# Reordering three stretches of a fused sparse-attention and bilinear feed-forward kernel on one NeuronCore

## Chip, cores and metric

One core of one Trainium2 chip runs the whole kernel. The metric is device time in microseconds (us). Engines are called as in the profile: PE (TensorE matmul), PEld (its weight loads), DVE (VectorE), ACT (ScalarE), POOL (GpSimd), SP (SyncE).

## What is computed

Inputs q, k, v have shape (8 batches, 8 heads, 576 positions, 64). Heads 0 to 3 see the last 32 positions ("local"), heads 4 to 7 see every earlier position with the same remainder modulo 32 ("strided"). The result, 4608 tokens of 512 numbers, goes through a feed-forward layer with a product instead of a nonlinearity.

```python
mask_local = (rel >= 0) & (rel < stride)                    # stride = 32
mask_strided = (rel >= 0) & (pos[None, :] % stride == pos[:, None] % stride)
scores = np.where(masks[None, :, :, :], scale * q @ k.T, -1000000000.0)
attn = softmax(scores)
x = (attn @ v).transpose(0, 2, 1, 3).reshape(B * S, H * D)
return (x @ w_a) * (x @ w_b) @ w_out                        # d_ff = 1536
```

## The kernel before

**Tiles.** The feed-forward layer runs over nine tiles t = 0 to 8 of 512 tokens. A tile has 16 slots: twelve `ffn_ab` (one block f of 128 of the 1536 middle columns each: eight matmuls of 512 columns, L546; ACT copies the a half, L563; DVE multiplies it with the b half into `pf`, L566 or L568) and four for the output multiplication. Attention of batch b lies between these slots, by the tables STEPS and LATER: in tile t of 2 to 6 the fifth values' step V5 of batch t+1 stands behind slot 11. The engines' instructions are issued in the order in which the program emits them (a manual schedule), so an instruction that waits holds all behind it on its engine.

**Output multiplication of tiles 2 to 8.** It is a fast matrix scheme with seven products of half size in place of eight; each product is, for q = 0 and 1, six matmuls of 256 columns (groups g = 0 to 5), accumulated in four PSUM banks a, b, c, d. The products are named 1 to 7. Products 3 and 4 read `pf` as it is. The others read sums of `pf` pieces, tile `ps`, five planes of six groups:

- plane 0, the diagonal sum, `fast_s(t, 0, ...)`, L579, read by product 1;
- planes 1 and 2, one instruction for both, `fast_s(t, 1, ...)`, L581, read by product 5 (plane 1) and product 2 (plane 2);
- planes 3 and 4, `fast_s(t, 2, ...)`, L583, read by products 6 and 7.

In tiles 2 to 7 (`y_plan`, matmuls at L650) the order is 3 4 1 7 5 2 6, each for both q. Groups 0 and 1 of the sums are made in earlier slots; groups 2 to 5 of the diagonal sum are emitted in slot 11, behind V5, whose last DVE part is two multiplications into xT (L471) that wait for two ACT steps (L464, L465). Groups 2 to 5 of planes 1 and 2 follow in slot 12. In tile 8 (`y_tail`, matmuls at L678) all seven products are done for q = 0 and then for q = 1, in the order 3 4 1 2 5 6 7. After product 4 of q = 0 comes `fast_s` for planes 1 and 2 of the last group, after product 1 that for planes 3 and 4. Product 2 accumulates onto bank b, product 5 onto a, 6 onto c. Behind product 2 ACT copies its bank (L693) and POOL subtracts it from the running sum (L694); behind product 5 the same at L698 and L699; behind 6 and 7 DVE finishes output quarters (L703, L706), which SP and ACT queues store.

**The first batch.** Batch 0 is worked through before any slot, in an order written out by hand, the string ORDER (L507). The steps are, for head pair c and unit u (units 0 to 3 local, 4 to 7 strided):

- Tk*c*p / Tq*c*p: PE transposes k or q (L264, L270); Tk*c*e by DVE (L281) and Tq*c*e by ACT (L285) copy them out;
- S*u*p: PE score product (L357; strided units first add the mask with two matmuls, L351), into the one buffer `st`; S*u*x: ACT exponential (L365); S*u*m: DVE mask (L375), local units only;
- V*u*p: PE product with v (L411), into one of two `o` banks; V*u*r and V*u*n: DVE reciprocal and multiplication (L419, L434), which set the bank free;
- X*c*p / X*c*e: PE transposes the result (L480), ACT or DVE copies it into xT (L496; X3: L493 and L494);
- G0 to G2: the strided mask on PE, DVE and POOL (G1 also issues many of POOL's loads); F0a to F1c: parts of the first two `ffn_ab`; Z: an ACT fill; *n: n filler matmuls (`spin`, L154).

S5, "the sixth score product", is unit 5; V2 and V3 are the last local values' products. POOL issues nearly all loads, in program order; weights come in `load_w` (L244) and `load_wo` (L247).

The softmax here doesn't subtract the row's maximum and nothing guards it: scores larger than these inputs give would overflow.

## Time and profile before

| | before |
|---|---|
| median of 4 runs | 333.03 us (332.79 to 338.19) |
| profiled execution: time, span | 332.82 us, 330.8 us |
| mean granted PE clock | 0.999 |
| PE busy | 324.5 us, 98% of the span |
| DVE, ACT, POOL busy | 80%, 61%, 53% |

The profiled execution's time is its span and 2.0 us around it. A timeline row is: start (us from the span's start), us from the first start to the last end, engine, line, operation, written tile <- read tiles, sizes, count, and in brackets how long the engine was idle before and what ended that. Instructions of one kind in a row are merged into one row. Matmuls overlap: a row of n matmuls lasts n - 1 start-to-start steps and one full duration.

### The profile page before, as it was taken

Reading aid. Unit: us, or ns where it says so; the run is one execution under the profiler, and the core shown is the slowest. Engines: PE = TensorE matmul, PEld = TensorE weight load, DVE = VectorE, ACT = ScalarE, POOL = GpSimd, SP = SyncE. Lnnn points to the kernel's source line nnn. Section 1 sums busy time; section 2 is a strip of 40 time slices with the busy share of each in tenths; the row PEclk is TensorE's granted clock in tenths of the full one; section 3 lists DMA queues with packets and bytes.
Section 4 is the critical chain, followed back from the end, with each engine's and each line's share of the span. In section 5 each row is a group of like instructions: output and inputs, shape, how many; then the busy total and the mean of one; then the engine's idle time right before and its main releaser. Section 6 shows DMA issues by size and latency. Waiting matters only on the chain.

```text
span 330.8 us, 7724 instructions
## 1 busy us (share of the span) xinstructions
PE 324.5 (98%) x2850; PEld 205.3 (62%) x2850; DVE 263.8 (80%) x500; ACT 201.9 (61%) x328; POOL 175.9 (53%) x296
## 2 busy tenths in 40 slices
PE   8999999999999999999999999999999999999995
PEld 6654555455555577556999985558555854584464
DVE  6867587778877999999999999999878845647662
ACT  5662956468777866787577757775777543313321
POOL 8946746399966655774577557854312031132021
PEclk9999999999999999999999999999999999999999
DMA  9999999599999599799898988998033022004004
GB/s 157 142 202 194 202 186 198 125 184 117 131 199 141 98 97 81 73 199 141 77 83 174 158 85 70 140 207 88 22 76 113 0 65 64 0 2 127 3 0 127
DMA packets 100662, 37.60 MB, mean 114 GB/s; under 512 B 77457, under 2 KB 97809, under 8 KB 100625
## 3 DMA queue, kind: packets, MB, share of 16 engines
q0 software_dynamic: 87760, 19.58, 64.8%
q1 hardware_dynamic: 12576, 17.34, 18.0%
q8 instruction: 22, 0.36, 0.5%
q10 hardware_dynamic: 288, 0.20, 0.2%
q14 instruction: 16, 0.12, 0.2%
HBM read 39.71 MB, written 9.44 MB: 149 GB/s over the span
## 4 chain that ended last, share of the span: by engine, by line
PE 81%; DMA 11%; POOL 4%; DVE 1%; issue 1%; POOLq 0%; ACT 0%; DVEq 0%
PE mm L546 50%; PE mm L650 17%; DMA vl<-in_v_dram 4%; PE mm L730 4%; PE o L455 4%; PE st L357 4%; DMA shared<-in_k_dram 3%; DMA wa_sb<-in_moe_w_a_dram 3%; PE mm L678 1%; POOL shared L196 1%; DMA natk<-in_k_dram 1%; POOL vl L223 1%; PE end L678 1%; POOL wa_sb L244 0%; DVE tk L300 0%
## 5 line engine op out<-in xcount | busy, mean ns | idle before, releaser
L546 PE MATMUL mm<-xT,wb_sb 128*128 128x512 bf16 (+1 forms) x472 | 110.3, 358 | 0.1
L546 PE MATMUL mm<-xT,wa_sb 128*128 128x512 bf16 (+1 forms) x472 | 110.4, 358 | 0.0
L563 ACT COPY a_sb<-mm 128x512 f32<-128x512 f32 x106 | 62.0, 585 | 49.0 <-PE mm L546 46.8
L546 PEld LDWEIGHTS <-wb_sb 128*128 128x128 bf16 x480 | 46.3, 98 | 44.5 <-issue 0.6
L879 POOL CAST pace<-pf 1x1 f32<-1x1 bf16 x84 | 29.2, 347 | 83.2 <-DVE pf L566 80.8
L566 DVE TENSOR_TENSOR pf<-a_sb,mm 128x512 bf16<-128x512 f32 x84 | 56.4, 671 | 17.0 <-PE mm L546 13.7
L546 PEld LDWEIGHTS <-wa_sb 128*128 128x128 bf16 x480 | 42.5, 98 | 31.3
L365 ACT ACTIVATE p<-st 128x576 bf16<-128x576 f32 (+1 forms) x64 | 41.6, 650 | 11.0 <-PE st L357 10.3
L464 ACT ACTIVATE xr<-o 64x576 f32<-64x576 f32 x48 | 31.1, 647 | 26.3 <-PE o L455 26.1
L650 PEld LDWEIGHTS <-ps 128*128 128x128 bf16 x360 | 34.1, 98 | 5.3 <-DVE ps L579 1.5
L465 ACT ACTIVATE xr<-xr 64x576 f32<-64x576 f32 x48 | 32.8, 683 | 1.5
L471 DVE TENSOR_TENSOR xT<-o,xr 64x288 bf16<-64x288 f32 x48 | 21.5, 447 | 8.0 <-ACT xr L465 7.0
L469 DVE TENSOR_TENSOR xT<-o,xr 64x288 bf16<-64x288 f32 x48 | 21.4, 446 | 7.5 <-ACT xr L465 7.0
L650 PE MATMUL mm<-wf,ps 128*128 128x256 bf16 x216 | 27.3, 273 | 0.1
L375 DVE TENSOR_TENSOR p<-p,mask_l 128x576 int16<-128x576 int16 x32 | 22.3, 698 | 2.8 <-ACT p L365 2.8
L730 PE MATMUL mm<-wo_sb,pf 128*128 128x512 bf16 x96 | 23.4, 379 | 0.0
L235 POOL DMA_DIRECT2D vs<-in_v_dram x24 | 19.6, 818 | 4.0 <-PE st L357 3.7
L568 DVE TENSOR_TENSOR pf<-a_sb,mm 128x512 bf16<-128x512 f32 x22 | 14.9, 676 | 7.5 <-ACT a_sb L563 5.9
L879 POOL COPY pace<-y_sb 1x1 f32<-1x1 f32 x16 | 2.8, 175 | 32.0 <-ACT y_sb L633 14.8
L211 POOL DMA_DIRECT2D ql<-in_q_dram x24 | 16.0, 665 | 5.7 <-DMA wo_sb<-in_moe_w_out_dram 3.7
L211 POOL DMA_DIRECT2D kl<-in_k_dram x24 | 16.1, 671 | 4.0 <-issue 3.8
L650 PE MATMUL mm<-wf,pf 128*128 128x256 bf16 x144 | 17.6, 273 | 0.0
(151 smaller groups left out, 501.7 us busy)
## 6 DMA issues: line engine op xcount, KB each, us to landing
out_dram<-y_sb SPq DMA_DIRECT2D x12, 512.0 KB, 5.1
vl<-in_v_dram POOLq DMA_DIRECT2D x7, 384.0 KB, 7.0
out_dram<-y_sb SPq DMA_DIRECT2D x10, 256.0 KB, 4.0
kl<-in_k_dram POOLq DMA_DIRECT2D x24, 72.0 KB, 3.4
ql<-in_q_dram POOLq DMA_DIRECT2D x24, 72.0 KB, 3.5
vs<-in_v_dram POOLq DMA_DIRECT2D x24, 72.0 KB, 3.6
wo_sb<-in_moe_w_out_dram POOLq DMA_DIRECT2D x4, 384.0 KB, 11.7
natk<-in_k_dram POOLq DMA_DIRECT2D x20, 72.0 KB, 3.4
```

Of the source, the lines that this page charges most:

```text
L211: nc.gpsimd.dma_start(out=t[32 * h:32 * h + 32], in_=src[b, h].rearrange("(i y) d -> y i d", y=32))
L365: nc.scalar.activation(p[:M, :, :W], st[:M, :, :W], ACT.Exp, scale=scale)
L375: nc.vector.tensor_tensor(pi, pi, mk, op=ALU.bitwise_and)
L464: nc.scalar.activation(r, sums, ACT.Ln)
L465: nc.scalar.activation(r, r, ACT.Exp, scale=-1.0)
L471: nc.vector.tensor_mul(dst.rearrange("d (p r) -> d p r", r=RS)[:, :, G * half:G * (half + 1)], o[:64, j, :W].rearrange("d (g p) -> d p g", ...
L546: nc.tensor.matmul(ps_[:, c0:c0 + n], lhsT=w[:, kk, 128 * f:128 * (f + 1)], rhs=xT[:, kk, x0:x0 + n], start=(kk == first and c0 == 0), sto ...
L563: nc.scalar.copy(a_sb, ab[0])
L566: nc.vector.tensor_mul(pf[:, f, :].rearrange("p (i a s) -> p a i s", i=2, s=16), halves(a_sb), halves(ab[1]))
L650: nc.tensor.matmul(bank[b][:, q], lhsT=lhs(g, q), rhs=rhs(g), start=new and q == 0 and g == 0, stop=g == FG - 1, skip_group_check=True)
L730: nc.tensor.matmul(y, lhsT=pf[:, f, 128 * j:128 * (j + 1)], rhs=wo_sb[:, f], start=(f == 0), stop=(f == FD - 1))
L879: nc.gpsimd.tensor_copy(pace, done)
```

## The change

Three orders are changed; nothing is computed differently and no instruction but fillers is added or removed. (1) In ORDER, V0n, S5p, S5x, X0p and X0e come before V2p; V2's and V3's steps, S6p, V4, X1p and V5p follow in a new order; G2 goes behind Tk2e; fillers go from *2 to *4 behind Tk0p, from *2 to *1 ahead of S4p, *2 are added ahead of V2p, and the *1 ahead of V7p and the *1 ahead of F0b go. (2) In tiles 2 to 7 the diagonal sum of groups 2 to 5 is emitted before the attention step behind slot 11. (3) In tile 8, q = 0, product 5 comes before product 2.

```diff
-        V1p S0m *2 S2p V1r S3m V0p S2x Tk3p V0r Tk3e *2 S4p S2m Tq3p S4x V1n Tq3e *4 V2p V0n S5p V2r V3p V2n S5x X0p V4p V3r
-        V3n X0e S6p V4r V5p V4n S6x X1p V5r S7p X1e V5n V6p S7x X2p V6r *1 V7p V6n X2e Z F0a V7r V7n *1 F0b X3p F1a X3e F0c
+        V1p S0m *2 S2p V1r S3m V0p S2x Tk3p V0r Tk3e *1 S4p S2m Tq3p S4x V1n Tq3e *4 V0n S5p S5x X0p X0e *2 V2p V2r V3p V2n
+        S6p V4p V3r V3n V4r V4n S6x X1p V5p V5r S7p X1e V5n V6p S7x X2p V6r V7p V6n X2e Z F0a V7r V7n F0b X3p F1a X3e F0c
...
-            for k in "3412567":
+            for k in ("3415267", "3412567")[q]:
...
+        soon = {16 * t + 11: [lambda t=t: fast_s(t, 0, slice(2, 6))] for t in FAST_Y[:-1]}
...
-            for slot, n, z0, z1 in ((4, 0, 0, 2), (6, 2, 0, 2), (8, 1, 0, 2), (10, 2, 2, 4), (11, 0, 2, 6), (11, 2, 4, 6),
+            for slot, n, z0, z1 in ((4, 0, 0, 2), (6, 2, 0, 2), (8, 1, 0, 2), (10, 2, 2, 4), (11, 2, 4, 6),
...
+            for f in soon.get(i, ()):
+                f()
             take(i)
```

## The prediction, made before the changed kernel was run

> **What bounds the kernel now.** I read the page's busy times first, then the waits of PE and PEld, then the timeline where those waits lie.

> ```profile
> PE 324.5 (98%) x2850; PEld 205.3 (62%) x2850; DVE 263.8 (80%) x500; ACT 201.9 (61%) x328; POOL 175.9 (53%) x296
> ...
> PEld L650 <- DVE ps L579: 1.5, 5, 0.3
> PEld L678 <- DVE ps L581: 0.5, 1, 0.5
> ```

> PE is busy for 98% of the span, and from 60 us on hardly anything keeps it waiting, so a reordering can only win the few waits left: five weight loads of product 1 waiting for the diagonal sum, one in the last tile, and what the first batch leaves. Those rows total the loader's idle time; what PE itself loses is read from the timeline. Tile 3, PE, then DVE:

> ```profile
> 190.77 1.24 PE L650 MATMUL mm<-wf,ps 128*128 128x256 bf16 x8
> 192.10 1.92 PE L650 MATMUL mm<-wf,ps 128*128 128x256 bf16 x16
> 193.85 0.71 PE L650 MATMUL mm<-wo_sb,ps 128*128 128x256 bf16 x5
> ...
> 188.65 0.68 DVE L566 TENSOR_TENSOR pf<-a_sb,mm 128x512 bf16<-128x512 f32 x1
> 189.48 0.91 DVE L471 TENSOR_TENSOR xT<-o,xr 64x288 bf16<-64x288 f32 x2 [0.16 <-ACT xr L465]
> 190.43 0.69 DVE L579 TENSOR_TENSOR ps<-pf 128x1024 bf16<-128x1024 bf16 x1
> 192.64 1.18 DVE L581 TENSOR_TENSOR ps<-pf 128x2048 bf16<-128x2048 bf16 x1
> ```

> Sixteen matmuls take 1.92 us, five 0.71: 0.11 each. Eight should take 0.71 + 3 x 0.11 = 1.04; product 1's first eight take 1.24. **0.20 is lost**, because the sum ends at 190.43 + 0.69 = 191.12, behind V5's L471. The last tile, products 1, 2 and 5, 6 on PE, then DVE:

> ```profile
> 318.43 0.82 PE L678 MATMUL mm<-wf,ps 128*128 128x256 bf16 x6
> 319.51 1.49 PE L678 MATMUL mm<-wo_sb,ps 128*128 128x256 bf16 x12 [0.27 <-DVE ps L581]
> 320.83 1.47 PE L678 MATMUL mm<-wf,ps 128*128 128x256 bf16 x12
> ...
> 319.04 0.42 DVE L581 TENSOR_TENSOR ps<-pf 128x512 bf16<-128x512 bf16 x1
> ```

> Six steps of 0.11 from 318.43 let product 2 start at 319.09; it starts at 319.51: **0.42 lost**. The start:

> ```profile
> 14.06 0.34 PE L411 MATMUL o<-vl,p 128*128 128x65 bf16 x6 [0.44 <-DMA vl<-in_v_dram]
> 14.24 0.41 PE L351 MATMUL st<-nmask,ident 72*128 72x288 bf16 x2
> 14.96 0.65 ACT L365 ACTIVATE p<-st 72x576 bf16<-72x576 f32 x1 [1.02 <-PE st L357]
> ...
> 47.01 1.67 PE L730 MATMUL mm<-wo_sb,pf 128*128 128x512 bf16 x6
> 49.26 1.46 PE L730 MATMUL mm<-wo_sb,pf 128*128 128x512 bf16 x6
> ```

> V2p at 14.06 waits for v, and S5p (14.24) and its exponential stand behind it. At 47.01 six matmuls take 0.21 more than six of the same kind at 49.26: the last quarter of w_out, issued by POOL at 34.89 with 12.9 us to landing (the longest of the four), lands at 47.8.

> **Diagonal sum first.** The sum reads block 11 of `pf`, so it starts when L566 ends, about 189.37 (in the last tile L579 starts 0.72 after L566, 317.39 to 318.11). It ends at 190.06, before product 1 begins at 190.77: the 0.20 goes, in the five tiles that the wait row counts, 1.0 in all. Queued behind it are V5's two L471, which move from 189.48 to 189.98 (step between neighbours 0.61) and end 0.5 later, at 190.9; they free bank o for V6's product, which starts at 191.84 now and about 191.6 then: 0.6 of cover, and what it lacks would be lost per tile. DVE loses its 0.16 idle, so L581 ends at about 193.72 instead of 193.82. Product 5 needs it at its third matmul, weights loaded from 193.96, then 193.76 at the earliest: just enough. I take 0.95 of the 1.0.

> [...] L579 at 190.43 lasts 0.69 and the next starts at 191.04, after 0.61, so here neighbours overlap by 0.08 and the row decides. [...]

> **Last tile.** L581 writes group 5 of planes 1 and 2 in one instruction. Product 2's first weight load already waits for it, though it reads group 0 of plane 2. Product 1's loads begin at 318.32, before L579's end at 318.40, so the wait isn't on the whole tile; it fits a wait on the range of addresses from the first to the last written, and plane 2's first groups lie within. Plane 1's groups 0 to 4 lie ahead of it, so product 5 can start at 319.09, and its sixth load comes at about 319.53, after L581's end at 319.46. The 0.42 goes. POOL then works for product 5 first and product 2 second, ready at about 321.8 (two of 0.7, from 320.4), so L703 slips from 321.74 to about 321.9; L706 at 322.40 is hardly touched, and the quarters of q = 0 are stored long before the last store. The end follows q = 1, whose order is the same: 0.42, less nothing. If the wait is for the tile after all, 0.

> **First batch.** Fillers: five take 0.67 and four 0.56, so 0.1 each at this clock; two more put Tq0p and all behind it 0.2 later, to V0p at 11.41. There Tk3p waits for k anyway (11.61, 0.17 idle on the loader): the 0.2 vanishes but for 0.1 on S4p, which waits for S2x. S5p then starts when S4x ends (12.77 + 0.1 + 0.65), 13.55 instead of 14.24. S5p takes 0.58 (14.24 to 14.82 now), X0p 0.37, two fillers 0.2: V2p starts at 14.70 instead of 14.06, **0.64 later**. From it V2n ends 1.16 on (15.86), V3n at 16.56. V4p waits for V2's bank (15.91), X1p and V5p for V3n (16.61); X1p 0.36 and V5p 0.44 give S7p at 17.41 instead of 17.20, and V7p, by S7's exponential, about 18.87 instead of 18.61. The score products' lead is eaten: S6p comes 0.8 earlier, but the values' chain on DVE is later and sets the end. One filler fewer behind V7p leaves F0c, and with it the tiles, **0.18 late** (bounds: 0, and the whole 0.64). G2's move hides behind Tk2p, for which Tk2e waits.

> PE's later waits up to 47 us are for DVE and ACT and move along; the one at 47.01 is for a landing. POOL's queue keeps it: the v loads behind V5p and V7p (18.15, 19.50) come 0.3 later at most, and POOL then idles 1.17 before 21.34. So lateness up to 0.21 costs nothing, and an earlier start would gain nothing either. I take 0, with 0 to 0.64 - 0.21 = +0.43.

> On the fillers' price: 23 at the very start take 4.45 us, 0.185 each, five from 6.59 on 0.10; I took 0.10, since the added ones come after 6 us. [...]

> **Sum.** -0.95 - 0.42 + 0 = -1.37. The profiled execution, 332.82, becomes 331.45; the median of the runs lies 0.21 above it (one run of 338.19 in it), so I say **331.6**.

> **Rivals.** *The wait moves to L581* (0.14): its slack at product 5 is 0.09 today (193.87 against 193.96); if DVE doesn't close its 0.16 idle, four tiles gain 0.09 each and only the sixth, where no transpose stands before L581, 0.2: 0.56 in place of 0.95, 332.0. *Product 5 waits as well* (0.09): the change doesn't do what it says in the tail, +0.42, 332.0; for it speaks that both planes come from one instruction, against it product 1's early loads. *The first batch is later than the cover* (0.13): +0.43, 332.0; for it the two o banks, which chain V2 to V7. *Slower* (0.07): the PE clock stays at half longer in the first batch, since its gaps change. Each us of PE work then costs 0.85 more (0.185 against 0.10). A start late by x costs x - 0.21, so it decides from x = 1.6, about 1.9 us of PE work at half clock, and with 3.0 us of it (x = 2.5) gives 332.82 - 1.37 + 2.3 = 333.8. Against it: fillers cost 0.10 throughout from 6 us, and gaps there are below 0.7.

> **Numbers.** My forecast has 0.57. About 0.2% (0.67 us) is what a measurement tells from no change. Below 332.4 lie the forecast and most of three rivals: faster 0.81. Two of the +0.4 cases together give about 332.4, and part of the start's lateness more: same 0.12. Slower 0.07. Low end: both full gaps (1.42) off the lowest run, 331.4, less 0.2 for run to run: 331.2. High end: two rivals at once, 332.4, and 0.1: 332.5.

> **What would show it.** Right: no wait on L579 at L650; product 1's eight in 1.04; last tile's product 5 starting 0.66 after product 1; F0c near 22.0 and the w_out wait gone or shorter; V2p near 14.7. Wrong: a wait on L581 at L650 or on V6's bank, F0c past 22.1 with PE behind after 48, or fillers of 0.185 after 6 us.

## The result and the profile after

The changed kernel took 331.95 us (median of 32 runs, 330.8 to 336.92) against 332.89 us for the kernel before (51 runs). The ratio is 0.997, 95% interval 0.9957 to 0.9983: 0.94 us faster, by the interval 0.6 to 1.4. The forecast was 331.6, range 331.2 to 332.5. Ratios here compare runs without a longer disturbance; each run's mean granted PE clock is told where it is part of the finding.

The profiled execution took 330.8 us with a span of 328.8, 2.0 less than before. The page's busy times, and the row on L471 of the waits of PEld:

```profile
PE 322.4 (98%) x2851; PEld 205.4 (62%) x2851; DVE 264.3 (80%) x500; ACT 202.1 (61%) x328; POOL 177.5 (54%) x296
...
PEld L455 <- DVE xT L471: 0.3, 1, 0.3
```

No row for L579 or L581 is left in that view, nor any wait of product 1, 2 or 5. The one wait for V5's L471 was there before, with the same 0.3. Tile 3 on PE, then DVE:

```profile
189.81 1.04 PE L650 MATMUL mm<-wf,ps 128*128 128x256 bf16 x8
190.69 0.42 PE L455 MATMUL o<-p,vs 72*128 72x72 bf16 x8
...
187.69 0.68 DVE L566 TENSOR_TENSOR pf<-a_sb,mm 128x512 bf16<-128x512 f32 x1
188.40 0.69 DVE L579 TENSOR_TENSOR ps<-pf 128x1024 bf16<-128x1024 bf16 x1
189.01 0.91 DVE L471 TENSOR_TENSOR xT<-o,xr 64x288 bf16<-64x288 f32 x2
```

The diagonal sum follows L566 and ends at 189.09, before product 1 begins; product 1's first eight take 1.04 where they took 1.24. The last tile, PE, then DVE:

```profile
316.87 0.82 PE L678 MATMUL mm<-wf,ps 128*128 128x256 bf16 x6
317.52 1.47 PE L678 MATMUL mm<-wo_sb,ps 128*128 128x256 bf16 x12
318.83 1.47 PE L678 MATMUL mm<-wf,ps 128*128 128x256 bf16 x12
...
317.48 0.41 DVE L581 TENSOR_TENSOR ps<-pf 128x512 bf16<-128x512 bf16 x1
```

Product 5 starts 0.65 after product 1, where product 2 started 1.08 after it; L581 runs beside product 5. The first batch, S5p, V2p (with V3p), X1p, S7p on PE, V3n on DVE, and the first `w_out` multiplications:

```profile
13.53 0.41 PE L351 MATMUL st<-nmask,ident 72*128 72x288 bf16 x2
14.57 0.53 PE L411 MATMUL o<-vl,p 128*128 128x65 bf16 x12
16.23 0.54 PE L480 MATMUL tp<-ident,xr 96*128 96x96 bf16 x6
17.08 0.41 PE L351 MATMUL st<-nmask,ident 72*128 72x288 bf16 x2
...
15.87 0.55 DVE L434 TENSOR_TENSOR xr<-o,rc 96x384 bf16<-96x384 f32 x1
...
46.83 1.50 PE L730 MATMUL mm<-wo_sb,pf 128*128 128x512 bf16 x6
48.90 1.46 PE L730 MATMUL mm<-wo_sb,pf 128*128 128x512 bf16 x6
```

S5p, emitted ahead of V2p now, starts at 13.53; behind V2p and its wait for v it had started at 14.24. F0c comes at 21.68 (21.86 before). The wait for `w_out` shrinks to 1.50 - 1.46 = 0.04, because its last quarter lands at 47.48 instead of 47.83.

Where the 2.0 went, by starting times of the same instructions in both traces: 0.54 by tile 1's last output multiplication (94.91 to 94.37; 0.35 of it is the earlier start and the earlier landing, 0.16 a single wait of a values' product at 80.9 that the second trace doesn't have), 1.02 more by product 1 of the last tile (318.43 to 316.87; all of it in product 1's first eight matmuls, 0.20 to 0.21 in each of the five tiles), 0.44 more by the start of q = 1 there (322.14 to 320.14), 0.02 behind. So this one execution shows the two expected gains, 1.46, and 0.54 of luck at the start: over all fourteen traces of this case the last quarter of `w_out` lands between 47.60 and 47.98 with the old ORDER and between 47.24 and 47.99 with the new one. The median shows less: 0.94. The experiments look for that difference.

### The profile page after: what moved, and what is told of

Same layout as the page of the kernel before. It is cut to its first block, busy times and chain, and to the rows that moved or that the text cites. A ratio compares the mean times of both kernels' runs of the same rounds, so it can differ in the third digit from the quotient of the medians.

```text
span 328.8 us, 7729 instructions
## 1 busy us (share of the span) xinstructions
PE 322.4 (98%) x2851; PEld 205.4 (62%) x2851; DVE 264.3 (80%) x500; ACT 202.1 (61%) x328; POOL 177.5 (54%) x296
## 4 chain that ended last, share of the span: by engine, by line
PE 81%; DMA 11%; POOL 4%; issue 1%; DVE 1%; POOLq 0%; ACT 0%; DVEq 0%
PE mm L546 50%; PE mm L650 17%; DMA vl<-in_v_dram 4%; PE mm L730 4%; PE o L455 4%; PE st L357 4%; DMA wa_sb<-in_moe_w_a_dram 3%; DMA shared<-in_k_dram 3%; PE mm L678 2%; POOL shared L196 1%; DMA natk<-in_k_dram 1%; POOL vl L223 1%; PE end L678 1%; POOL wa_sb L244 0%; DVE tk L300 0%
## 5 line engine op out<-in xcount | busy, mean ns | idle before, releaser
L546 PE MATMUL mm<-xT,wb_sb 128*128 128x512 bf16 (+1 forms) x472 | 110.3, 358 | 0.1
L546 PE MATMUL mm<-xT,wa_sb 128*128 128x512 bf16 (+1 forms) x472 | 110.4, 358 | 0.0
L880 POOL CAST pace<-pf 1x1 f32<-1x1 bf16 x84 | 31.3, 373 | 83.2 <-DVE pf L566 80.7
L546 PEld LDWEIGHTS <-wb_sb 128*128 128x128 bf16 x480 | 46.3, 98 | 44.6 <-issue 0.6
L566 DVE TENSOR_TENSOR pf<-a_sb,mm 128x512 bf16<-128x512 f32 x84 | 56.4, 671 | 17.0 <-PE mm L546 13.7
L546 PEld LDWEIGHTS <-wa_sb 128*128 128x128 bf16 x480 | 42.5, 98 | 31.3
L365 ACT ACTIVATE p<-st 128x576 bf16<-128x576 f32 (+1 forms) x64 | 41.6, 649 | 10.3 <-PE st L357 9.7
L650 PEld LDWEIGHTS <-ps 128*128 128x128 bf16 x360 | 34.5, 98 | 3.9
L465 ACT ACTIVATE xr<-xr 64x576 f32<-64x576 f32 x48 | 32.8, 683 | 1.5
L471 DVE TENSOR_TENSOR xT<-o,xr 64x288 bf16<-64x288 f32 x48 | 21.5, 448 | 6.3 <-ACT xr L465 5.1
L650 PE MATMUL mm<-wf,ps 128*128 128x256 bf16 x216 | 26.4, 273 | 0.0
L730 PE MATMUL mm<-wo_sb,pf 128*128 128x512 bf16 x96 | 23.3, 380 | 0.0
L211 POOL DMA_DIRECT2D kl<-in_k_dram x24 | 16.1, 670 | 4.0 <-issue 3.9
L650 PE MATMUL mm<-wf,pf 128*128 128x256 bf16 x144 | 17.6, 273 | 0.0
```

The costliest lines, as they stand in the source:

```text
L211: nc.gpsimd.dma_start(out=t[32 * h:32 * h + 32], in_=src[b, h].rearrange("(i y) d -> y i d", y=32))
L365: nc.scalar.activation(p[:M, :, :W], st[:M, :, :W], ACT.Exp, scale=scale)
L465: nc.scalar.activation(r, r, ACT.Exp, scale=-1.0)
L471: nc.vector.tensor_mul(dst.rearrange("d (p r) -> d p r", r=RS)[:, :, G * half:G * (half + 1)], o[:64, j, :W].rearrange("d (g p) -> d p g", ...
L546: nc.tensor.matmul(ps_[:, c0:c0 + n], lhsT=w[:, kk, 128 * f:128 * (f + 1)], rhs=xT[:, kk, x0:x0 + n], start=(kk == first and c0 == 0), sto ...
L566: nc.vector.tensor_mul(pf[:, f, :].rearrange("p (i a s) -> p a i s", i=2, s=16), halves(a_sb), halves(ab[1]))
```

## The experiments

**Each part alone, and the two late parts together.** 12 runs each, side by side with the kernel before at 332.83 (35 runs).

The new ORDER and nothing else (edit against the changed kernel):

```diff
-            for k in ("3415267", "3412567")[q]:
+            for k in "3412567":
...
-        soon = {16 * t + 11: [lambda t=t: fast_s(t, 0, slice(2, 6))] for t in FAST_Y[:-1]}
...
-            for slot, n, z0, z1 in ((4, 0, 0, 2), (6, 2, 0, 2), (8, 1, 0, 2), (10, 2, 2, 4), (11, 2, 4, 6),
+            for slot, n, z0, z1 in ((4, 0, 0, 2), (6, 2, 0, 2), (8, 1, 0, 2), (10, 2, 2, 4), (11, 0, 2, 6), (11, 2, 4, 6),
```

> Only the first batch's new order. Theory W (each part removes the waits that it touches and the gains add up; the first batch's order is worth little because PE then waits for the last quarter of w_out anyway): 0.0 to -0.4 us, S7p and F0c about 0.2 earlier than in the kernel before, and the start of the 28th output matmul row behind w_out unchanged against the landing (landing + 0.04). Rival L (the first batch's order is what took 0.4 from the sum of 1.37, since the median gain was 0.94): +0.4 us, F0c late, PE behind after 48 us with no wait for w_out. No wait on L579 is removed by it: L650's five waits of 0.3 stay.

Measured: 333.17 (332.15 to 333.75), ratio 0.9995 [0.9966, 1.0024]: no gain. Its profiled execution (333.62 us, span 331.6) shows more. Stretches of its trace, columns: stretch, length, busy time of PE, PEld, DVE, ACT, POOL with counts, granted PE clock, DMA share, GB/s; then the L546 matmuls of the first feed-forward parts (counts, ns min/median/max), in this kernel:

```profile
14.80:18.25 3.45, 3.21 (x83) 2.37 (x80) 3.24 (x9) 2.36 (x4) 2.70 (x4) 1.00 1.35 185
18.25:21.66 3.41, 3.17 (x29) 1.77 (x29) 1.66 (x4) 1.72 (x3) 0.68 (x2) 0.50 1.31 203
...
L546 PE MATMUL ab<-xT,wa_sb x3: 383/634/634, 19.5 to 21.9; 128*128 128x512 bf16 x3
```

and in the changed kernel's profiled execution:

```profile
14.80:18.25 3.45, 3.23 (x84) 2.39 (x80) 3.13 (x8) 2.36 (x5) 2.66 (x4) 1.00 1.39 191
18.25:21.66 3.41, 3.29 (x42) 1.94 (x43) 2.21 (x5) 2.27 (x4) 0.76 (x2) 1.00 1.31 203
...
L546 PE MATMUL ab<-xT,wa_sb x6: 376/377/383, 19.0 to 21.7; 128*128 128x512 bf16 x6
```

The two show nearly the same busy times up to 18.25. Then the one has PE's clock granted at 0.50 for 3.41 us, and a matmul of 512 columns takes 634 ns instead of 377. F0c comes at 23.08 (21.68 in the changed kernel, 21.86 before), the wait for `w_out` is gone, and PE is 1.02 late behind it against the kernel before (the first transposes L264 after 48 us: 49.63 against 48.61). So one such stretch costs 1.40 of start against the changed kernel's execution and 1.22 against the kernel before's, of which 0.20 is covered.

The diagonal sum alone (against the kernel before):

```diff
+        soon = {16 * t + 11: [lambda t=t: fast_s(t, 0, slice(2, 6))] for t in FAST_Y[:-1]}
...
-            for slot, n, z0, z1 in ((4, 0, 0, 2), (6, 2, 0, 2), (8, 1, 0, 2), (10, 2, 2, 4), (11, 0, 2, 6), (11, 2, 4, 6),
+            for slot, n, z0, z1 in ((4, 0, 0, 2), (6, 2, 0, 2), (8, 1, 0, 2), (10, 2, 2, 4), (11, 2, 4, 6),
...
+            for f in soon.get(i, ()):
+                f()
```

> Only the diagonal sum ahead of the attention step. Theory W: -0.95 us (0.19 to 0.20 in each of five tiles), no loader wait on L579, product 1's first eight in 1.04 us. Rival L: the same -0.95. Rival M (the wait moves to L581): -0.5 us and a wait of L650 on L581 in four tiles.

Measured: 331.85 (331.45 to 335.03), ratio 0.9964 [0.9934, 0.9994], 0.98 under before. No wait on L579 in its trace. The profiled execution was the 335.03: `v` landed late (PE sat idle 1.79 for it until 15.04) and the clock was at half from 17.54 to 24.36.

The last tile's order alone (against the kernel before):

```diff
-            for k in "3412567":
+            for k in ("3415267", "3412567")[q]:
```

> Only product 5 ahead of product 2 for q = 0 in the last tile. Theory W: -0.42 us, product 5 starts 0.66 after product 1, the stretch from product 1 of q = 0 to the span's end falls from 12.4 to 12.0 us. If the time does not follow, that stretch's last store would have to wait for something else: 0.

Measured: 332.74 (331.88 to 336.63), ratio 1.0007 [0.9969, 1.0045]. The interval is wider than the effect: 4 of the 12 runs had a lowered clock; the other eight have a median of 332.45. The trace shows the effect itself:

```profile
318.55 0.82 PE L678 MATMUL mm<-wf,ps 128*128 128x256 bf16 x6
319.20 1.47 PE L678 MATMUL mm<-wo_sb,ps 128*128 128x256 bf16 x12
```

0.65 from product 1 to product 5, and 11.92 from product 1 to the end of the span where before has 12.40. The timing neither shows nor denies it.

Both late parts, with the old ORDER (against the changed kernel; its other ORDER lines go back in the same way):

```diff
-        V1p S0m *2 S2p V1r S3m V0p S2x Tk3p V0r Tk3e *1 S4p S2m Tq3p S4x V1n Tq3e *4 V0n S5p S5x X0p X0e *2 V2p V2r V3p V2n
+        V1p S0m *2 S2p V1r S3m V0p S2x Tk3p V0r Tk3e *2 S4p S2m Tq3p S4x V1n Tq3e *4 V2p V0n S5p V2r V3p V2n S5x X0p V4p V3r
```

> All but the first batch's order. Theory W: -1.37 us, as the changed kernel within 0.3. Rival L: -1.37, and the changed kernel 0.4 slower than this one.

Measured: 331.48 (330.97 to 332.25), ratio 0.9944 [0.9917, 0.9971], 1.35 under before. The whole forecast gain, without part 1. The changed kernel's first 32 runs lie 0.47 above this, as rival L has it, but its later two sets of 12 (below) lie at 331.45 and 331.81, so medians alone do not settle what part 1 costs.

**What the runs' clocks say.** A stretch of 3.41 us at half clock lowers the mean granted clock of a 330 us run by 0.5 x 3.41 / 330 = 0.005. Counting runs below 0.9965 (none lies between 0.995 and 0.997): the kernel before 9 of 93, the changed kernel 21 of 56 (13 of the first 32; the counts of its later runs are below), the new ORDER alone 2 of 12, the three kernels above with the old ORDER 1, 4 and 1 of 12. In those first 32 the nineteen with the clock up have a median of 331.51, the thirteen others 332.78.

The depth of the mean clock follows the length of the fall in the five traces that have one: 0.995, 0.994 and 0.992 with 3.41 us at half, 0.988 with 6.83, 0.982 with 10.24. The clock also drops behind the last matmuls (granted at 0.50 from 330.26 on in the trace before, whose last matmul ends at 327.00, and from 328.06 on in the changed kernel's, 325.00); runs that are not low have means of 0.997 to 1.000. From these numbers the author estimates how long a fall was: of the changed kernel's 21 low runs 18 have 0.993 or 0.994, one stretch; of the 9 of the kernel before only one has (0.994), the others 0.978 to 0.990, two stretches or more. So it is the single stretch that the new ORDER brings, 18 of 56 against 1 of 93; longer falls are rare with either, 3 and 8. Whether the new ORDER keeps PE less busy depends on the stretch: between 14.80 and 18.25 it does (3.23 us against 3.45), between 11.40 and 14.80 it keeps PE busier (the kernel before, then the changed one, whose row for 14.80 stands above).

```profile
11.40:14.80 3.40, 2.84 (x54) 1.85 (x50) 2.28 (x8) 1.74 (x3) 3.40 (x6) 1.00 1.38 120
14.80:18.25 3.45, 3.45 (x93) 2.73 (x88) 2.94 (x7) 2.77 (x5) 2.20 (x4) 1.00 1.39 193
...
11.40:14.80 3.40, 3.29 (x63) 2.46 (x64) 2.15 (x6) 2.38 (x5) 3.40 (x6) 1.00 1.49 148
```

The new theory: part 1 leaves PE's work in a part of the first batch thinner, so that the clock more often falls for one stretch; that takes the median of the first 32 runs up by about 0.4. Its rival: the falls come by chance, whatever the order. One kernel adds work to PE where it waits, two take some away.

Five fillers at waits of PE, in the changed kernel:

```diff
-        S6p V4p V3r V3n V4r V4n S6x X1p V5p V5r S7p X1e V5n V6p S7x X2p V6r V7p V6n X2e Z F0a V7r V7n F0b X3p F1a X3e F0c
+        S6p *3 V4p V3r V3n V4r V4n S6x *1 X1p V5p V5r S7p X1e V5n V6p S7x *1 X2p V6r V7p V6n X2e Z F0a V7r V7n F0b X3p F1a X3e F0c
```

> The changed kernel with five more fillers in the first batch, put where PE waits: three ahead of V4p, one ahead of X1p, one ahead of X2p. Theory G (the new order leaves a stretch at 15 to 19 us that is so thin in matmul columns, 51 to 59% of a 3.41 us window, that the PE clock falls to half for one window in 13 of 32 runs of the changed kernel, at about 1.0 us each; the fillers bring it to 62% or more): at most 1 run in 12 with a mean clock under 0.9965, median 331.4 to 331.5 us, 0.4 below the changed kernel. Rival N (fillers do nothing but delay PE, and the low clock is chance of the chip): 4 to 5 runs in 12 under 0.9965, median 332.0 to 332.4.

Measured: 331.50 (331.17 to 332.64), ratio 0.9945 [0.9917, 0.9972], one run of 12 below 0.9965. In the stretch that was thin PE now shows as busy throughout:

```profile
14.80:18.25 3.45, 3.45 (x85) 2.81 (x82) 2.66 (x8) 2.38 (x4) 2.12 (x4) 1.00 1.40 196
```

The changed kernel again, side by side with it:

> The changed kernel once more, on the same chip as the two others. Theory G: 4 to 5 runs of 12 under 0.9965, the others at 331.5, the whole at about 331.9. Rival N (chance of the chip on the first day): under 0.9965 as seldom as the kernel before, 1 in 12, median 331.5.

Measured: 331.45 (330.93 to 333.33), ratio 0.9946 [0.9914, 0.9977]; three of 12 runs low, at a median of 333.25, the others 331.27. Too close to the kernel with fillers to part the two by time, so both were run a second time, beside the opposite edit: the twelve fillers between S3x and V2p taken out of the changed kernel.

```diff
-        C0 Tk0p *4 Tq0p Tk0e Tq0e *5 Tk1p S1p M Tq1p S1x Tk1e *4 G0 Tq1e S0p S1m G1 C1 Tq2p S0x Tk2p Tq2e S3p Tk2e G2 S3x *3
-        V1p S0m *2 S2p V1r S3m V0p S2x Tk3p V0r Tk3e *1 S4p S2m Tq3p S4x V1n Tq3e *4 V0n S5p S5x X0p X0e *2 V2p V2r V3p V2n
+        C0 Tk0p *4 Tq0p Tk0e Tq0e *5 Tk1p S1p M Tq1p S1x Tk1e *4 G0 Tq1e S0p S1m G1 C1 Tq2p S0x Tk2p Tq2e S3p Tk2e G2 S3x
+        V1p S0m S2p V1r S3m V0p S2x Tk3p V0r Tk3e S4p S2m Tq3p S4x V1n Tq3e V0n S5p S5x X0p X0e V2p V2r V3p V2n
```

> The changed kernel without the twelve fillers that stand between S3x and V2p in the first batch (*3, *2, *1, *4, *2). Theory G (the clock falls after a 3.41 us window that is thin in matmuls; where the window lies against the first batch differs from run to run): nearly every window between 9 and 19 us now has under 55% of matmul columns, so at least 8 of 12 runs lie under a mean clock of 0.9965, and the median is 332.3 us or more. The runs whose clock stays up are not slower than the changed kernel's, 331.2 to 331.5, since the fillers stand before waits. Rival N (the fall has nothing to do with the fillers): 3 to 4 runs of 12, median 331.5 or, with PE earlier by what the fillers took, less.

Measured: 334.69 (333.93 to 336.45), ratio 1.0044 [1.0019, 1.007], all 12 runs low (0.974 to 0.984). With less work for PE the kernel is 3.2 to 3.5 us slower than the changed kernel's runs with the clock up. Its stretches:

```profile
11.40:14.80 3.40, 3.04 (x51) 1.94 (x47) 2.17 (x6) 1.98 (x4) 3.40 (x6) 0.72 1.42 140
14.80:18.25 3.45, 3.45 (x62) 2.88 (x60) 2.13 (x6) 2.01 (x4) 2.25 (x4) 0.50 1.36 187
```

The clock is at half from 12.87 to 23.11, although PE shows as busy throughout the second stretch.

The kernel with the five fillers again:

> The kernel with five more fillers at PE's waits once more. Theory G: at most 2 runs of 12 under 0.9965, median 331.4 to 331.5 us. Rival N: 3 to 5 of 12.

Measured: 331.47 (330.99 to 332.06), ratio 0.995 [0.993, 0.997], none of 12 low.

The changed kernel a third time:

> The changed kernel beside the two others, for their share of runs with a low clock. Theory G: 3 to 5 of 12 under 0.9965, the others at 331.3 to 331.5 us. Rival N: as e12_fillers_again.

Measured: 331.81 (330.65 to 333.48), ratio 0.9961 [0.9936, 0.9986]; five of 12 low at a median of 332.82, the others 331.18. Its profiled execution was at half clock from 19.48 to 22.89. Over both sets: with the five fillers 1 of 24 runs low, without 8 of 24. The rival falls: more fillers, fewer falls; no late fillers, falls in every run.

Four fillers taken from the old ORDER, with both late parts in:

```diff
-        V1p S0m *2 S2p V1r S3m V0p S2x Tk3p V0r Tk3e *2 S4p S2m Tq3p S4x V1n Tq3e *4 V2p V0n S5p V2r V3p V2n S5x X0p V4p V3r
+        V1p S0m *2 S2p V1r S3m V0p S2x Tk3p V0r Tk3e *2 S4p S2m Tq3p S4x V1n Tq3e V2p V0n S5p V2r V3p V2n S5x X0p V4p V3r
```

> The old first-batch order with parts two and three, but without the four fillers between Tq3p and V2p, which stand before a wait for v and so cost no time. Theory G: windows that begin from 10.5 to 13.4 us fall from 62 to 67% to 51 to 56%, so the clock falls in 8 to 11 runs of 12, median about 332.5 us, 1.0 above the same kernel with its fillers (331.48). Rival N: as with them, 1 run in 12, 331.5.

Measured: 331.26 (330.77 to 335.44), ratio 0.9967 [0.9926, 1.0008]; four of 12 runs low, three of them at 334.4 to 335.4. More than the 1 of 12 with the `*4` in, though twelve runs each don't tell 4 from 1, and far from the eight or more expected: the account of how thin is too thin was wrong in size.

**The wait of product 2 in the last tile.** Is it on the range of addresses, or on both planes as such? In the kernel before, planes 2 and 1 of the last group by two instructions, plane 2 first:

```diff
-                            fast_s(t, 1, slice(FG - 1, FG))
+                            for z in (1, 0):
+                                nc.vector.tensor_tensor(last[:, 1 + z], pl[:, 0, z], pl[:, 1, z], op=ALU.add)
```

> The kernel before, but in the last tile the sum of the last group of planes 1 and 2 is made by two instructions, plane 2 first, in place of one for both; order 3 4 1 2 as before. Theory R (product 2's first load waits because one instruction that writes both planes is taken to cover all addresses from the first to the last): product 2 then starts 0.66 us after product 1, as product 5 does in the changed kernel, with no wait on its first load. Rival T (a reader waits for any write to the tile): product 2's first load waits for both instructions, 0.5 us or more.

Measured: 332.26, span 330.3, one execution. PE and the two DVE instructions:

```profile
318.22 0.82 PE L678 MATMUL mm<-wf,ps 128*128 128x256 bf16 x6
318.97 1.47 PE L678 MATMUL mm<-wo_sb,ps 128*128 128x256 bf16 x12
318.84 0.48 DVE L690 TENSOR_TENSOR ps<-pf 128x256 bf16<-128x256 bf16 x2
```

Product 2 now starts 0.75 after product 1 instead of 1.08, while the last group of its own plane is still being made (the first of the two instructions runs from 318.84 to 319.12). So neither the tile nor the plane as such holds it. In the kernel before, its first weight load came at 319.51, 0.05 behind the end of the one instruction for both planes (319.46); what it reads is the same in both kernels, and product 5 of the changed kernel starts at 317.52, while that instruction runs (317.48 to 317.89). The three traces fit a wait on the span of addresses that one instruction writes; that is the author's inference from them. What is left above 0.65 ends with L685, which frees bank b at 318.92; product 5, on bank a, does not have this wait.

**The other half of the last tile.** Product 5 before 2 for q = 1 too:

```diff
-            for k in ("3415267", "3412567")[q]:
+            for k in "3415267":
```

> The changed kernel with product 5 ahead of product 2 for q = 1 too. PE gains the 0.09 us for which product 2 waits for bank b. But POOL then finishes the sum that product 6's L703 needs second, about 0.7 us later, and behind L703 stand the last two L706 on DVE and the last stores: from the start of q = 1 to the span's end 8.66 us before, about 0.3 more with it. If POOL is not on that path, 0.09 less.

Measured: 332.86, span 330.86, with one stretch at half clock in its start (18.43 to 21.84), so only the tail is read. From q = 1's start to the end it takes 330.86 - 321.43 = 9.43; in the changed kernel 328.81 - 320.14 = 8.67: 0.76 lost, more than twice the 0.3 expected. POOL, then DVE:

```profile
325.81 0.73 POOL L694 TENSOR_TENSOR ya<-ya,y_sb 128x256 f32<-128x256 f32 x1 [0.38 <-ACT y_sb L693]
326.56 0.42 DVE L703 TENSOR_TENSOR y_sb<-mm,ya 128x256 f32<-128x256 f32 x1 [2.54 <-POOL ya L694]
```

The output quarter of L703 waits 2.54 for POOL's subtraction behind product 2, and comes 5.13 after q = 1's start, where it came 4.29 after it (324.43 - 320.14). Behind q = 0 there is time to catch up; behind q = 1 nothing follows.

## Why the prediction was right, and where it wasn't

**Diagonal sum, -0.95.** Right: five waits gone, 1.02 in the traces (the forecast took 0.05 off its 1.0 without need), 0.98 in the runs of this part alone (interval 0.2 to 2.2). V6's product did not come late for its bank. The rival that the wait moves to L581 fell: no such wait in any trace with the new place. The step of 0.61 between neighbours on DVE, read from the row before, held: L471 starts 0.61 behind L579, which lasts 0.69 (188.40 and 189.01).

**Last tile, -0.42.** Right in the trace (0.43), and its reason, a wait on a range of addresses, fits most of it: product 2 starts 1.08 behind product 1 with one instruction for both planes and 0.75 with two. About 0.1 of the 0.43 is another wait, which the prediction didn't name: product 2 alone would have come 0.75 behind product 1, for bank b, as the kernel with the planes apart shows; product 5 comes 0.65 behind it. That product 5 waits as well fell. By time alone it is not shown.

**First batch, 0.** With the clock up the sum fits, but two steps were wrong. V2p was forecast at 14.70 and came at 14.57 (X0p and two fillers 0.46, not 0.57). "X1p and V5p for V3n (16.61)" was the larger miss: X1p's first three transposes read only what V2n wrote, so X1p starts at 16.23, before V3n ends at 16.42, and S7p follows at 17.08 instead of 17.41. F0c came 0.18 early, not 0.18 late, in this pair of executions; with the clock up it lies between 21.58 and 22.29 in four executions with the old ORDER and at 21.68 and 22.18 in two with the new one, so the forecast of 0.18 is below what traces can tell, and that the sum fits is in part luck. An early start ends at the landing of `w_out`, as the prediction said. With the clock up part 1 moves nothing that these runs can tell: side by side, the new ORDER alone has a median of 332.96 and the kernel before 332.83; the changed kernel's such runs have medians of 331.51, 331.27 and 331.18, the late parts with the old ORDER 331.35. With all runs counted the term was not 0: in the first 32 runs the falls of the clock take the median up by 0.44.

**The slower rival** is where the working failed. It named what the runs show, PE's clock at half in the first batch (granted at 0.50 for 3.41 us in the execution of the new ORDER alone), at a chance of 0.07 and 333.8, as if it came in all runs or none. It comes in 21 of 56 runs. The argument against it, "fillers cost 0.10 throughout from 6 us, and gaps there are below 0.7", looked at one trace with the clock up, and at single gaps. In the execution of the new ORDER alone the longest loss on PE in the 3.41 us ahead of the fall is 0.37 (the longest idle time in its timeline there is 0.21, at 15.63), and the clock fell: no gap near 0.7 was needed. The price for each us of work held, the length didn't: at 0.185 for 0.10 a stretch of 3.41 us with PE always at work loses 1.57, and F0c came 1.40 later; but 3.0 us of work, as the prediction had it, fill 5.6 us at half clock, where 18 of the 21 low runs have the mean clock of one fall of 3.41 (0.993 or 0.994).

**Sum.** -1.37 forecast; -1.35 with the late parts alone; -1.4 for the changed kernel's runs with the clock up (331.51 against 332.89). The stated 331.6 was a little low by its own sum (331.45 + 0.21 = 331.66). That the 32 runs came out at 331.95 is the share of runs with a stretch at half clock: without them it is 331.51.

**A steadier version** is the changed kernel with the five fillers at PE's waits: 331.50 and 331.47, range's top 332.64, where the changed kernel has 331.45 and 331.81, top 333.48, side by side; over 24 runs each the means are 331.56 and 331.84, a difference whose 95% interval, about -0.1 to 0.7, still holds 0. The fillers are not quite free: with the clock up alone these kernels have 331.49 and 331.47 against 331.27 and 331.18. The late parts with the old ORDER do as well in their 12 runs (331.48). Both beat the kernel before clearly; over the changed kernel the lead is the rarer fall, and small.

**Open.** How full a stretch must be. Cut the start of each trace into seven stretches of 3.41 us from the moment when its clock comes on (below), and weigh each matmul by its columns at the full clock's step (512 columns in 0.215 us, as from 23.08 to 24.37 in the execution of the new ORDER alone, six steps). Then the stretches just ahead of the five falls in the traces (new ORDER alone, diagonal sum alone, both halves, the changed kernel a third time, no late fillers) were filled to 54 to 58%; three others, at 54, 56 and 57%, saw no fall, and none fell at 63% or more. Matmul records can be missing from a trace (the new ORDER alone lists seven of the first parts' matmuls with `wa_sb`, the traces before and after eight), so this is rough, and the run with fewer fillers shows that it does not forecast well. Weighing by the rows of the array in use too puts the five at 31 to 36% and all others at 36% or more; this weighing was chosen afterwards and is not tested.

## What to carry to other kernels

When an engine is 98% busy, price its remaining waits from start-to-start steps of equal instructions; the two such sums here (the five waits and the last tile's) held to 0.1 us. Moving work forward in the first batch gained nothing behind the landing of `w_out`, which was later anyway (with the clock up 332.96 for the new ORDER alone, side by side with 332.83), and with the new ORDER single falls of the granted clock came in 18 of 56 runs against 1 of 93. Fillers at PE's waits there took the low runs from 8 of 24 to 1 of 24 (their price here: 0.2 to 0.3 us with the clock up); look at each run's mean granted clock, not at the median alone. In the last tile product 2 started 1.08 us behind product 1 with one instruction writing two strided planes, 0.75 with the planes written apart, and product 5, whose first pieces lie outside the span written, 0.65 in its place: where a reader of addresses in between waits like this, write the planes apart, or read the plane outside the span first.

## What the hardware showed that was not expected

That the same kernel falls in some runs and not in others would fit steps of 3.41 us that meet the first batch at a different place in each run. This is the author's estimate, from the five traces with the new ORDER and its fillers as they are: the clock came on at 3.62 and 3.79 where it didn't fall, the stretch at 14 us being filled to 67 and 65%; it came on at 4.60, 4.78 and 5.83 where it fell, at 18.25, 18.43 and 19.48, and the stretch ahead of the fall, from 14.8 to 16.1 us on, was filled to 54 to 57%. Five executions are few, and no run set the moment on purpose, so it is not shown.
